# Strided attention and a squared-ReLU layer: where the strided V is spread, and an early load's place in the queue

## The chip, the cores and the metric

The kernel runs on one core of one Trainium2 chip. A core has a matrix engine (TensorE, PE in the profile, with its weight loads as PEld), a vector engine (VectorE, DVE), an activation engine (ScalarE, ACT), a general engine (GpSimd, POOL) and a queue engine that only issues transfers (SyncE, SP). Each engine works through its own instructions in order. Transfers (DMA) are issued from the queues of SP and POOL; those of POOL can change the type on the way, here float32 in memory to bfloat16 on the core. The metric is the device time of one execution in microseconds.

## The reference

For 8 batches and 8 heads of 576 positions with 64 numbers each, the reference computes masked attention: heads 0 to 3 see the last 32 positions ("local"), heads 4 to 7 see earlier positions with the same remainder by 32 ("strided"). Its output, 4608 tokens of 512 numbers, goes through a layer with a squared ReLU.

```
mask_local = (rel >= 0) & (rel < stride)
mask_strided = (rel >= 0) & (pos[None, :] % stride == pos[:, None] % stride)
...
attn = np.exp(scores)
attn = attn / (np.sum(attn, axis=-1, keepdims=True) + 1e-09)
return np.matmul(attn, v).astype(np.float32)
...
h = x @ w_in          # 4608x512 by 512x2048
r = np.maximum(h, 0.0)
g = r * r
return (g @ w_out).astype(np.float32)
```

## The kernel before

Work is cut into 32 units, four per batch: two heads each, the first two units of a batch local, the last two strided. Unit u is of batch u // 4. For each unit the attention goes through steps: T (TensorE transposes q and k, in early batches), S (scores into PSUM banks `pt`, ScalarE takes the exponential into `e`, VectorE multiplies by the mask, L361, or L427 in the paired form SS), D (probabilities by V, L488, then on VectorE a reciprocal L500 and a product L501 into `x_l` or `x_s`; two parts for local, three for strided units), E (transposes x into `xt`).

The layer is cut into 9 chunks of 512 tokens: `mm1(c, i)`, 16 per chunk (L548; ReLU on ScalarE L554; square on VectorE L557 into `g_sb`), and `mm2(c, i)`, 16 per chunk (L588, four matmuls each). A written list of "groups", one mm1 or mm2 each, drives the second part of the kernel, and the attention's steps are put between groups by weights (`due`). `hooks` holds further work by group number: `second(n, ...)` and `at(n, ...)` put a function ahead of group n, after that group's attention steps. The program is emitted in this order, and each engine keeps it.

Strided V needs a layout in which 64 numbers of a position are followed by a column of ones, with a pitch of 72: the tile `vs` (72 partitions x 16 x 72). The data come as dense rows of 512 numbers into `v_st` and are spread from there into `vs` by `cast_v_str` (L255), once for each of the two strided units of a batch.

- Batches 0 and 1 take another way (`load_v_str_first`).
- Batches 2, 3 and 4: one transfer on POOL's queue per batch, float32 to bfloat16 (`load_v_str_sw`, L232); the spreading is on GpSimd, bfloat16 to bfloat16 (`cast_v_str_pair`).
- Batches 5, 6 and 7 (`LB` = 5 on): two float32 transfers on SP's queue (`load_v_str`, L248); GpSimd spreads and casts. The local V of these batches is loaded likewise (`load_v_local`, L216) and cast on GpSimd (`cast_v_local`, L223 and L224).

At group 29 POOL gets a long list: it holds until batch 2's transposes are done (`hold_pool`), issues V of batch 2, q and k rows of batch 3 (`rows(3)`, L133), V of batch 3, the copies of strided q and k of batch 3 (`q_d`, `k_d`, L168), and then spreads V of batches 2 and 3. Two memsets of `vl_st` (L864) follow. At group 51 the same comes for batch 4, with its spreading at group 60.

From batch 5 on, `plan` puts `loads_qk(b)` (loads, the copies `q_d` and `k_d`, casts of q and k on GpSimd, L143) and later `loads_v(b)` at group `n0`. For batches 5, 6 and 7, `n0` is 80, 112 and 144, and `loads_qk` comes at groups 67, 92 and 124.

`v_st` has two buffers and `vs` four slots, so batches b and b + 2 share them.

At the start, `loads_1` issues on POOL's queue: q and k of batch 1's local units, the four quarters of w_out (`load_w_out`, L264) and V of batch 1 among them. Part p of mm2 reads quarter p of w_out; chunk 0 runs its parts in turn for four row blocks, and unit 4's D at group 19 is the first reader of batch 1's local V.

Of the kernel before, what the change touches and what calls it, by code (L numbers as in the profile page):

```python
# [8 lines left out]
FP32 = mybir.dt.float32  # L9
# [5 lines left out]
def kernel(  # L15
# [9 lines left out]
    nc = tc.nc  # L25
    B, H, S, D = q.shape
# [7 lines left out]
    NJ = 8  # L34
    RH = STRIDE // NJ
    SP_ = RH * NA
# [7 lines left out]
    v_st = ctx.enter_context(tc.tile_pool(name="v_st", bufs=2))  # L44
# [54 lines left out]
    units = [(b, p) for b in range(B) for p in range(H // 2)]  # L99
    st = {}  # L100
# [24 lines left out]
    def load_qk_local_sw(b, us, names="qk"):  # L125
        n = 2 * len(us)
        for name, src in (("q", q), ("k", k)):
            if name not in names:
                continue
            t = qk_st.tile([QL, 2, 6 * D], FP32, name=f"{name}_st")  # L130
            t = t.rearrange("p h c -> p (h c)").bitcast(BF16)[:, 0:6 * D * n].rearrange("p (h c) -> p h c", h=n)
            h0 = 2 * units[us[0]][1]
            nc.gpsimd.dma_start(out=t, in_=src[b, h0:h0 + n].rearrange("h (p j) d -> p h (j d)", j=6))  # L133
            for i, u in enumerate(us):
                st.setdefault(u, {})[name + "f"] = t[:, 2 * i:2 * i + 2]

    def cast_qk_local(u, copies, names="qk"):
        s = st[u]
        for name, copy in zip("qk", copies):
            if name not in names:  # L140
                continue
            t = qk_in.tile([QL, 6, 2, D], BF16, name=f"{name}_l")
            copy(t.rearrange("p j h d -> p h j d"),  # L143
                 s[name + "f"].rearrange("p h (j d) -> p h j d", j=6))
            s[name] = t

    def load_qk_str(b, names="qk", room=None):
        for i, (name, src) in enumerate((("q", q), ("k", k))):
            if name not in names:
                continue  # L150
            if room is None:
                t = qk_st.tile([QL, 2, 6 * D], FP32, name=f"{name}_st")
                t = t.rearrange("p h c -> p (h c)").bitcast(BF16).rearrange("p (c x) -> p c x", c=3)
            else:
                t = room[0:QL, 3 * i:3 * i + 3, :]
            nc.gpsimd.dma_start(out=t, in_=src[b, 4:8].rearrange("h (p j) d -> (h p) (j d)", j=NJ)
                                .rearrange("(c r) x -> r c x", r=QL))
            big[b, name] = t
# [6 lines left out]
    def cast_str_dram(b):  # L165
        for name, src in (("q", q), ("k", k)):
            t = dram.tile([4 * SP_, NJ * D], BF16, name=f"{name}_d")
            nc.gpsimd.dma_start(  # L168
                out=t.rearrange("(x y) c -> x (y c)", x=16),
                in_=src[b, H // 2:H].rearrange("h (x y) d -> (h x) (y d)", x=4))  # L170
            big[b, name] = t
# [24 lines left out]
    def transpose_local(u):  # L196
        s = st[u]
        for name in "qk":
            if name == "k":
                full = kTl[v_slot(u)]  # L200
                dst = full[:, 32:32 + S]
            else:
                full = dst = qkT.tile([128, S], BF16, name="qk"[u % 2] + "T")
            nc.sync.dma_start_transpose(out=dst.rearrange("c (t p) -> c t p", p=QL),
                                        in_=s[name].rearrange("p t h d -> p (t h d)"))
            s[name + "T"] = full

    def v_slot(u):
        b, p = units[u]
        return (b * 2 + p % 2) % NV  # L210

    def load_v_local(u, eng):
        b, p = units[u]
        t = vl_sts[p]
        for hh in range(2):
            eng.dma_start(out=t[32:128, NL * hh:NL * (hh + 1), :],  # L216
                          in_=v[b, 2 * p + hh].rearrange("(t p) d -> p t d", p=QL))
        st.setdefault(u, {})["vf"] = t
# [10 lines left out]
    def load_v_str_sw(b):  # L229
        t = v_st.tile([SP_, 2, NJ * D], FP32, name="v_st")  # L230
        t = t.rearrange("p h c -> p (h c)").bitcast(BF16).rearrange("p (h c) -> p h c", h=4)
        nc.gpsimd.dma_start(out=t, in_=v[b, 4:8].rearrange("h (p j) d -> p h (j d)", j=NJ))  # L232
        for i in range(2):
            st.setdefault(4 * b + 2 + i, {})["vf"] = t[:, 2 * i:2 * i + 2]

    def load_v_local_sw(b, u0=0, nu=2):
        i = (2 * b + u0) % NV
        t = vl_all[:, i:i + nu].rearrange("p u h t d -> p (u h t) d")[:, :, 0:D]
        src = v[b, 2 * u0:2 * (u0 + nu)].rearrange("h (t p) d -> p (h t) d", p=QL)
        nc.gpsimd.dma_start(out=t[32:128], in_=src)  # L240
        nc.gpsimd.dma_start(out=t[0:32, 1:2 * nu * NL], in_=src[64:96, 0:2 * nu * NL - 1])
        for u in range(nu):
            st.setdefault(4 * b + u0 + u, {})["v"] = vls[i + u]

    def load_v_str(u, eng):
        b, p = units[u]
        t = v_st.tile([SP_, 2, NJ * D], FP32, name="v_st")
        eng.dma_start(out=t, in_=v[b, 2 * p:2 * p + 2]  # L248
                      .rearrange("h (p j) d -> p h (j d)", j=NJ))
        st.setdefault(u, {})["vf"] = t  # L250

    def cast_v_str(u, copy=None):
        s = st[u]
        t = vss[v_slot(u)]
        (copy or nc.gpsimd.tensor_copy)(t[:, :, 0:D], s["vf"].rearrange("p h (j d) -> p (h j) d", d=D))  # L255
        s["v"] = t

    def load_w_in(i):
# [3 lines left out]
    def load_w_out(i):  # L262
        c = slice(4 * i, 4 * (i + 1))
        nc.gpsimd.dma_start(out=w_out_b[:, c, :], in_=w_out_v[:, c, :])  # L264
# [174 lines left out]
    def load_v_str_first(b):  # L439
        nc.gpsimd.dma_start(  # L440
            out=vs0.rearrange("p u n d -> p (u n d)").rearrange("p (h c) -> p h c", h=4),
            in_=v[b, 4:8].rearrange("h (p j) d -> p h (j d)", j=NJ))
# [223 lines left out]
    def loads_1():  # L666
        load_qk_local_sw(1, (4, 5), "q")
        load_qk_local_sw(1, (4, 5), "k")
        load_w_out(0)
        load_w_out(1)  # L670
        load_v_local_sw(1)
        load_qk_str(1)
        load_w_out(2)
        load_v_str_first(1)
        load_w_out(3)

    def hold_pool(b):
        nc.gpsimd.tensor_copy(held, came[b])

    def cast_v_str_pair(b):  # L680
        for u in (4 * b + 2, 4 * b + 3):
            cast_v_str(u)

    def loads_qk(b):
        for i in range(2):
            load_qk_local(4 * b + i, nc.sync)
        if b == LB:
            hold_pool(b - 1)
        cast_str_dram(b)
        for i in range(2):  # L690
            cast_qk_local(4 * b + i, pool2)

    def loads_v(b):
        for i in range(2):
            load_v_local(4 * b + i, nc.sync)
        for i in range(2):
            load_v_str(4 * b + 2 + i, nc.sync)
        for i in range(2):
            cast_v_local(4 * b + i)
        for i in range(2):  # L700
            cast_v_str(4 * b + 2 + i)

    nc.scalar.preload_act_table_set("natural_log_exp_and_others")
    load_qk_local(0, nc.sync)
# [106 lines left out]
    def at(n, fn):  # L811
        hooks.setdefault(n, []).append(fn)

    def plan(b, g0, g1, n0=None):
        if b < LB:
            at(g0, lambda: transpose_str(b))
            for i in range(2):
                copies = dve2 if b == 2 else (nc.scalar.copy, nc.vector.tensor_copy)
                at(g1 + (4 if b > 2 else 2) * i, lambda u=4 * b + i, c=copies: cast_qk_local(u, c))
            return  # L820
        g = g0 + (g1 - g0) * 45 // 100
        tr, tl = max(g + 8, g0 + (g1 - g0) * 8 // 10), (g + 14, g + 18)
        at(g, lambda: loads_qk(b))
        at(tr, lambda: transpose_str(b))
        at(n0, lambda: loads_v(b))
        for i in range(2):
            at(tl[i], lambda u=4 * b + i: transpose_local(u))

    def second(n, *fns):
        for fn in fns:  # L830
            at(n, fn)

    def D_all(u):
# [23 lines left out]
    rows = lambda b: (lambda: load_qk_local_sw(b, (4 * b, 4 * b + 1)))  # L857
    second(14, rows(2), lambda: cast_str_dram(2))
    plan(2, 28, 28)
    second(29, lambda: hold_pool(2), lambda: load_v_local_sw(2), lambda: load_v_str_sw(2), rows(3),  # L860
           lambda: load_v_local_sw(3), lambda: load_v_str_sw(3), lambda: cast_str_dram(3),
           lambda: cast_v_str_pair(2), lambda: cast_v_str_pair(3))
    for t in vl_sts:
        second(29, lambda t=t: nc.gpsimd.memset(t[0:32], 0.0))  # L864
    done_prev, g_prev = 0, 32
    plan(3, 42, 46)
    second(51, lambda: hold_pool(3), rows(4), lambda: load_v_local_sw(4), lambda: load_v_str_sw(4),
           lambda: cast_str_dram(4))
    second(60, lambda: cast_v_str_pair(4))
    plan(4, 64, 61)  # L870
    for b in range(2, B):
        g_end, s_end = ready.get(b, starts[b]), ends[4 * b + 3]
# [50 lines left out]
```

## Time and profile before

| | us |
|---|---|
| median of 8 runs | 308.86 |
| lowest, highest | 308.46, 310.24 |
| the profiled execution's own time | 310.24 |
| its span, first to last instruction | 308.5 |
| PE busy in the span | 298.9 |
| DVE, ACT, POOL busy | 160.7, 166.1, 74.5 |
| strided V spread on GpSimd, 12 instructions | 6.7 + 7.0 |

The page gives busy times for the whole span. PE's line shows how little it stands; what matters are the places where it does. The table by stages gives each engine's busy time in a stretch; the list of waits tells which engine's instruction ended a wait; the timeline shows single instructions with start and duration, and in brackets the idle time of the engine before it with what ended it. A duration on DVE or POOL can hold time in which the instruction stood and did not work, so the same instruction at two places is worth comparing.

### The profile page before, as it was taken

What the parts mean: (1) busy time and instruction counts of PE and PEld (TensorE: products, weight loads), DVE (VectorE), ACT (ScalarE), POOL (GpSimd) and SP (SyncE); (2) the same over time, 40 slices, a digit from 0 to 9 for tenths busy, and PEclk for the clock granted to TensorE, in tenths of its full rate; (3) what the DMA queues carried; (4) which work ended last, traced back from release to release, by engine and by line L of the source; (5) the groups of instructions that cost most, each with busy time, mean ns of one, the idle gap of its engine ahead of it and who ended that gap; (6) DMA issues with size and microseconds to landing.
All of it is one profiled execution on the core that took longest, in us unless ns stands there. A gap on an engine that the chain in (4) does not pass through costs nothing.

```text
span 308.5 us, 6092 instructions
## 1 busy us (share of the span) xinstructions
PE 298.9 (97%) x2368; PEld 149.3 (48%) x2368; DVE 160.7 (52%) x406; ACT 166.1 (54%) x335; POOL 74.5 (24%) x103
## 2 busy tenths in 40 slices
PE   7989999999999999999999999999999999999995
PEld 2544564544554554445445554444444444444444
DVE  4557656478777875665748586563422222222200
ACT  4748738786577765554646555464434344444311
POOL 8853210664512324440443052000000000000000
PEclk9999999999999999999999999999999999999999
DMA  8999997999999989998999592221230001000121
GB/s 158 149 203 205 189 208 150 224 165 160 139 194 185 214 167 211 187 178 194 214 195 204 122 185 70 72 55 53 83 96 36 34 35 36 34 34 34 59 79 69
DMA packets 85908, 40.74 MB, mean 132 GB/s; under 512 B 69784, under 2 KB 79544, under 8 KB 85688
## 3 DMA queue, kind: packets, MB, share of 16 engines
q1 hardware_dynamic: 59560, 25.37, 36.7%
q0 software_dynamic: 26320, 14.99, 35.7%
q8 instruction: 18, 0.29, 0.4%
q14 instruction: 10, 0.08, 0.1%
HBM read 37.63 MB, written 13.57 MB: 166 GB/s over the span
## 4 chain that ended last, share of the span: by engine, by line
PE 84%; DVE 8%; DMA 4%; ACT 1%; POOL 1%; issue 1%; SPq 0%; DVEq 0%; ACTq 0%
PE ph L548 36%; PE py L588 27%; PE ph L588 6%; PE pt L588 3%; PE pt L488 3%; DMA w_in_b<-in_moe_w_in_dram 3%; DVE g_sb L557 2%; PE pt L347 2%; PE pt L548 1%; DMA k_st<-in_k_dram 1%; DVE x_l L501 1%; PE pt L291 1%; DVE e L361 1%; PE pt L570 1%; DVE k_l L143 1%; DVE x_s L501 1%
## 5 line engine op out<-in xcount | busy, mean ns | idle before, releaser
L548 PE MATMUL ph<-xt,w_in_b 128*128 128x512 bf16 x552 | 139.8, 379 | 0.0
L554 ACT ACTIVATE r<-ph 128x512 bf16<-128x512 f32 x138 | 82.3, 597 | 94.3 <-PE ph L548 92.7
L557 DVE TENSOR_TENSOR g_sb<-r 128x512 bf16<-128x512 bf16 x144 | 65.1, 453 | 104.7 <-ACT r L554 103.8
L588 PE MATMUL py<-w_out_b,g_sb 128*128 128x512 bf16 x400 | 102.7, 379 | 0.0
L548 PEld LDWEIGHTS <-w_in_b 128*128 128x128 bf16 x576 | 52.3, 98 | 55.5 <-DMA w_in_b<-in_moe_w_in_dram 0.7
L588 PEld LDWEIGHTS <-g_sb 128*128 128x128 bf16 x560 | 51.4, 98 | 56.3 <-issue 0.4
L326 ACT ACTIVATE e<-pt 128x288 bf16<-128x288 f32 (+1 forms) x86 | 30.5, 408 | 8.8 <-PE pt L347 8.7
L588 PE MATMUL ph<-w_out_b,g_sb 128*128 128x512 bf16 x112 | 28.2, 379 | 0.0
L488 PEld LDWEIGHTS <-e 128*128 128x128 bf16 (+1 forms) x384 | 20.1, 97 | 15.4 <-DVE e L361 1.1
L592 ACT COPY y<-py 128x512 f32<-128x512 f32 x25 | 14.7, 586 | 6.3 <-PE py L588 6.3
L501 DVE TENSOR_TENSOR x_s<-pt,rinv 72x384 bf16<-72x384 f32 (+1 forms) x33 | 16.7, 505 | 1.1
L501 DVE TENSOR_TENSOR x_l<-pt,rinv 96x384 bf16<-96x384 f32 x25 | 13.8, 554 | 0.9
L500 DVE RECIPROCAL rinv<-pt 96x6 f32<-96x6 f32 (+2 forms) x58 | 10.7, 184 | 5.9 <-PE pt L488 5.7
L223 POOL CAST vl<-vl_st 128x768 bf16<-128x768 f32 x6 | 5.3, 891 | 31.7 <-DMA vl_st<-in_v_dram 20.0
L488 PE MATMUL pt<-vs,e 72*128 72x65 bf16 x174 | 11.1, 194 | 1.3 <-DVE e L361 0.7
L423 ACT ACTIVATE e<-pt 72x504 bf16<-72x504 f32 (+3 forms) x25 | 10.9, 482 | 0.6 <-PE pt L411 0.6
L588 PE MATMUL pt<-w_out_b,g_sb 128*128 128x512 bf16 x48 | 11.2, 379 | 0.0
L255 POOL COPY vs<-v_st 72x1024 bf16<-72x1024 bf16 x6 | 6.7, 1138 | 15.4 <-DMA v_st<-in_v_dram 15.4
L361 DVE TENSOR_TENSOR e<-e,mask_full 128x576 bf16<-128x576 bf16 x20 | 9.0, 450 | 1.8 <-ACT e L326 1.6
L361 DVE TENSOR_TENSOR e<-e,mask_str 72x576 bf16<-72x576 bf16 x16 | 7.8, 494 | 3.8 <-ACT e L326 3.7
L488 PE MATMUL pt<-vl,e 128*128 128x65 bf16 x150 | 8.7, 193 | 0.0
L592 ACT COPY y<-ph 128x512 f32<-128x512 f32 x7 | 4.1, 581 | 7.0 <-PE ph L588 7.0
(132 smaller groups left out, 237.1 us busy)
## 6 DMA issues: line engine op xcount, KB each, us to landing
out_dram<-y SPq DMA_DIRECT2D x35, 256.0 KB, 2.9
w_out_b<-in_moe_w_out_dram POOLq DMA_DIRECT2D x4, 512.0 KB, 14.7
q_d<-in_q_dram POOLq DMA_DIRECT2D x6, 288.0 KB, 8.2
k_d<-in_k_dram POOLq DMA_DIRECT2D x6, 288.0 KB, 9.5
q_st<-in_q_dram SPq DMA_DIRECT2D x12, 144.0 KB, 3.6
k_st<-in_k_dram SPq DMA_DIRECT2D x12, 144.0 KB, 5.7
vl_st<-in_v_dram SPq DMA_DIRECT2D x12, 144.0 KB, 4.1
v_st<-in_v_dram SPq DMA_DIRECT2D x6, 288.0 KB
```

Of the source, the lines that this page charges most:

```text
L255: (copy or nc.gpsimd.tensor_copy)(t[:, :, 0:D], s["vf"].rearrange("p h (j d) -> p (h j) d", d=D))
L326: nc.scalar.activation(e[0:kn, lo:lo + S // 2], pss[row][half][0:kn, 0:S // 2], AF.Exp, scale=scale)
L361: nc.vector.tensor_tensor(x, x, m, op=ALU.mult)
L423: nc.scalar.activation(o, x, AF.Exp, scale=scale)
L488: nc.tensor.matmul(po[:, n - n0, :], e[0:kn, pos(n):pos(n) + 128], rhs[0:kn, src(n), 0:D + 1], start=True, stop=True)
L500: nc.vector.reciprocal(rinv[0:w, 0:m], po[0:w, 0:m, D:D + 1])
L501: nc.vector.tensor_tensor(x, po[0:w, 0:m, 0:D], rinv[0:w, 0:m].to_broadcast([w, m, D]), op=ALU.mult)
L548: nc.tensor.matmul(ph, w_in_b[:, kk, 128 * ff:128 * (ff + 1)], xt[kk][:, 512 * c:512 * (c + 1)], start=(kk == order[0]), stop=(kk == order ...
L554: nc.scalar.activation(r, ph, AF.Relu)
L557: later(1, lambda: nc.vector.tensor_tensor(g[:, ff, :], r, r, op=ALU.mult))
L588: nc.tensor.matmul(py, g[:, ff, 128 * j:128 * (j + 1)], w_out_b[:, ff, :], start=(ff == 0), stop=(ff == 15))
L592: nc.scalar.copy(y, py)
```

## The change

Four edits. `load_v_str` and its six transfers on SP's queue go; batches 5 to 7 use `load_v_str_sw` in `loads_qk`, issued on POOL's queue behind `q_d` and `k_d`. The spreading of all six batches goes from GpSimd to VectorE, one unit per group: batch 2 at groups 43 and 44, batch 3 at 56 and 57, batch 4 at 72 and 73, batches 5 to 7 at `n0 + 1` and `n0 + 2`. At group 29, `rows(3)` goes ahead of batch 2's `load_v_str_sw`. In `loads_1`, V of batch 1's local units goes ahead of w_out's second quarter.

```diff
-    def load_v_str(u, eng):
...
-    def cast_v_str(u, copy=None):
+    def cast_v_str(u, copy):
         s = st[u]
         t = vss[v_slot(u)]
-        (copy or nc.gpsimd.tensor_copy)(t[:, :, 0:D], s["vf"].rearrange("p h (j d) -> p (h j) d", d=D))
+        copy(t[:, :, 0:D], s["vf"].rearrange("p h (j d) -> p (h j) d", d=D))
         s["v"] = t
...
         load_w_out(0)
+        load_v_local_sw(1)
         load_w_out(1)
-        load_v_local_sw(1)
         load_qk_str(1)
...
-    def cast_v_str_pair(b):
-        for u in (4 * b + 2, 4 * b + 3):
-            cast_v_str(u)
...
         cast_str_dram(b)
+        load_v_str_sw(b)
         for i in range(2):
             cast_qk_local(4 * b + i, pool2)
...
         for i in range(2):
             load_v_local(4 * b + i, nc.sync)
         for i in range(2):
-            load_v_str(4 * b + 2 + i, nc.sync)
-        for i in range(2):
             cast_v_local(4 * b + i)
-        for i in range(2):
-            cast_v_str(4 * b + 2 + i)
...
         at(n0, lambda: loads_v(b))
         for i in range(2):
+            at(n0 + 1 + i, lambda u=4 * b + 2 + i: cast_v_str(u, nc.vector.tensor_copy))
             at(tl[i], lambda u=4 * b + i: transpose_local(u))
...
-    second(29, lambda: hold_pool(2), lambda: load_v_local_sw(2), lambda: load_v_str_sw(2), rows(3),
-           lambda: load_v_local_sw(3), lambda: load_v_str_sw(3), lambda: cast_str_dram(3),
-           lambda: cast_v_str_pair(2), lambda: cast_v_str_pair(3))
+    second(29, lambda: hold_pool(2), lambda: load_v_local_sw(2), rows(3), lambda: load_v_str_sw(2),
+           lambda: load_v_local_sw(3), lambda: load_v_str_sw(3), lambda: cast_str_dram(3))
+    for b, n in ((2, 43), (3, 56), (4, 72)):
+        for i in range(2):
+            second(n + i, lambda u=4 * b + 2 + i: cast_v_str(u, nc.vector.tensor_copy))
...
-    second(60, lambda: cast_v_str_pair(4))
```

## The prediction

> **What bounds the kernel now.** First I read the page's busy times: TensorE (PE) is busy for 97% of the span, at a granted clock of 9 tenths or more in every slice.
>
> ```profile
> PE 298.9 (97%) x2368; PEld 149.3 (48%) x2368; DVE 160.7 (52%) x406; ACT 166.1 (54%) x335; POOL 74.5 (24%) x103
> ```
>
> So no engine's sum of work matters, only PE's idle time: 308.5 - 298.9 = 9.6 us. The table by stages places it.
>
> ```profile
> 0.00:30.00 30.00, 26.12 (x262) 13.44 (x263) 17.05 (x58) 18.45 (x39) 19.05 (x34) 1.00 1.19 178
> 66.00:80.00 14.00, 12.69 (x137) 6.68 (x134) 12.17 (x30) 10.32 (x24) 5.57 (x6) 1.00 1.23 159
> 94.00:100.00 6.00, 5.54 (x45) 2.52 (x44) 4.90 (x11) 4.64 (x10) 2.21 (x2) 1.00 1.03 162
> 180.00:187.00 7.00, 6.60 (x71) 3.34 (x68) 6.23 (x15) 3.98 (x8) 6.00 (x6) 1.00 0.93 150
> ```
>
> Columns: stretch, its length, busy time of PE, weight load, VectorE (DVE), ScalarE, GpSimd (POOL). The start has 3.9 us of idle PE and the tail (300 to 308.5, not shown) 3.5; the change reaches neither. Between, 1.31 us is lost in 66-80, 0.46 in 94-100 and 0.40 in 180-187: there DVE is busy for 87, 82 and 89%, and POOL works on elements. PE's waits in those stretches all end on DVE:
>
> ```profile
> PE pt L488 <- DVE e L361: 0.7, 1, 0.7
> PE pt L347 <- DVE x_s L501: 0.6, 1, 0.6
> PE pt L488 <- DVE x_s L501: 0.5, 1, 0.5
> PE pt L411 <- DVE x_s L501: 0.4, 1, 0.4
> ```
>
> The timelines (start, duration) tell why DVE is late. POOL, then DVE, then PE:
>
> ```profile
> 73.16 2.25 POOL L255 COPY vs<-v_st 72x1024 bf16<-72x1024 bf16 x2 [5.19 <-DMA v_st<-in_v_dram]
> 75.36 1.40 POOL L864 MEMSET vl_st<- 32x768 f32 x2
> 95.03 2.21 POOL L255 COPY vs<-v_st 72x1024 bf16<-72x1024 bf16 x2 [8.99 <-DMA v_st<-in_v_dram]
> ```
> ```profile
> 73.45 1.05 DVE L361 TENSOR_TENSOR e<-e,mask_str 72x576 bf16<-72x576 bf16 x1
> 75.60 1.38 DVE L143 COPY k_l<-k_st 96x768 bf16<-96x768 bf16 x1
> 90.40 0.35 DVE L143 COPY k_l<-k_st 96x768 bf16<-96x768 bf16 x1
> 95.42 0.92 DVE L557 TENSOR_TENSOR g_sb<-r 128x512 bf16<-128x512 bf16 x1 [0.71 <-ACT r L554]
> 96.27 1.19 DVE L143 COPY k_l<-k_st 96x768 bf16<-96x768 bf16 x1
> ```
> ```profile
> 74.56 0.30 PE L488 MATMUL pt<-vs,e 72*128 72x65 bf16 x4 [0.74 <-DVE e L361]
> 79.12 0.28 PE L347 MATMUL pt<-qT,kTl 64*128 64x96 bf16 x5 [0.57 <-DVE x_s L501]
> 98.39 0.35 PE L488 MATMUL pt<-vs,e 72*128 72x65 bf16 x6 [0.46 <-DVE x_s L501]
> ```
>
> The same copy takes 0.35 us with POOL idle and 1.38 or 1.19 beside a POOL copy or memset; a mask product takes 1.05 instead of its 0.45, a square 0.92 instead of 0.42. PE then stands.
>
> **The change, part by part.** All durations are of the profiled execution (310.24 us, span 308.5); the median of the eight runs is 308.86, so I carry the difference over to the median and keep a wide range for it.
>
> *Copies of batches 2 to 4 go to DVE.* POOL loses six copies of 1.03 to 1.26 us; DVE gains six. Price of one on DVE: k_l's 0.35 us for 768 columns, by 1024/768, is 0.47 as a whole, and a fixed part would make it less: I take 0.40. Bounds: 0.35 below; above, 1.33 us, if it ran at the 0.75 us per 576 columns of the copies from PSUM. `v_st` and `vs` lie in SBUF in runs of 64 numbers, as k_l's tiles do, so the k_l row is the near one.
>
> Batch 2 (group 43, after unit 8's first x_l, which ends at 67.76) also gains a wait. Its transfer is now issued behind q and k rows of batch 3 (`rows(3)`), so it is fifth in the POOL queue, and lands about where k's rows land now:
>
> ```profile
> k_st<-in_k_dram POOLq DMA_DIRECT2D x1, 288.0 KB, 8.3
> ```
>
> 60.19 + 8.3 = 68.5 (it landed at 58.78 + 6.9 = 65.7). DVE stands from 67.76 to 68.5. Queued behind it: the square of group 43, x_l of unit 8, masks of unit 9, for which PE's L488 at 70.10 waits. I walk DVE's rows on from there, start to start (copy 0.33, square 0.34, reciprocal 0.21, product 0.48, mask 0.36): the first mask of unit 9 ends at 70.7 instead of 69.32 (PE +0.6). The queue stays packed, the idle 0.40 before 71.02 is used up, and mask_str, now 0.45 instead of 1.05, ends at 74.8 instead of 74.50 (PE +0.27). Then k_l costs 0.35 instead of 1.38, since POOL's memsets now follow its DMA issues at 64.5 to 66; x_s of unit 10 ends at 78.3 instead of 79.06, and the bank is free before PE comes. The matmul of 79.12 starts at 78.64: **-0.47**. Bounds: if the data were there at 67.8, PE would gain about 1.2 here (-0.47 - 0.74); each us of later landing costs one us, so +1.0 at a landing of 70.
>
> Batch 3 (groups 56, 57; about 84.0 and 85.0): 0.33 each; DVE's idle 0.34, 0.17 and 0.77 before 85.24, 87.09 and 88.64 covers them. 0, with 0.66 above if that cover were gone, and no gain, as only work is added. Batch 4 (groups 72, 73; about 103.2 and 105.6): idle 0.57, 0.44 and 0.49 before 104.52, 106.43 and 108.75 covers them. 0, above 0.66.
>
> At 94-100 POOL's copies of batch 4 are gone: the square gives back 0.50 and k_l 0.84. The x_s that ends at 98.34 would end near 97.6; PE came at 96.90 + 4 x 0.216 = 97.77 and started at 98.39: **-0.62**, which is all of that wait; 0 is the other bound.
>
> *Batches 5 to 7.* SP loses six issues of 0.30 to 1.09 us, POOL six casts of 1.04 to 1.28 and gains three issues of 0.76; DVE gains six copies of 0.40. Only batch 5 is close: POOL issues at 105.85, behind k_d (105.36 + 6.3 = 111.7 landed), so it lands near 113.2 (1.5 behind, as batch 4's V, 84.23 + 10.7, is behind its neighbour now), and DVE asks at group 81, near 113. Behind it stand a square (four r buffers, eight groups of nearly 1 us of slack) and unit 17's x_l at 115.48; DVE has 0.80 and 0.50 idle before 114.56 and 115.48. 0, above 0.5. The issue pushes q_l and k_l casts of batch 5 by 0.76, of which the waits of 0.32 and 3.81 before 108.30 and 112.94 take all. Batches 6 and 7 land some 10 us ahead of groups 113 and 145. Without POOL's cast at 184.47, DVE's rows up to 186.6 get back 0.14 (square 0.56 at 185.47 against 0.42); the v_l casts at 180.68 stay, but their loads no longer share queues with two v_st loads. Take **-0.2**; bounds 0 and the whole stall, -0.57.
>
> *Start-up.* V of batch 1 lands now at 20.26 + 16.9 = 37.2 and 21.55 + 16.4 = 38.0; L488 reads it at 37.94, with no idle PE. After the swap the queue, which serves in order of issue, brings V by 35.3 and w_out's second quarter by 38.0 instead of 34.5 (19.26 + 15.2). The mm2 of part 1 that reads it starts at 39.49: 1.5 us spare. On POOL each issue waits for the landing eight issues earlier; the waits reshuffle between three neighbours, and q_d's issue at 38.42 stays. 0; bounds -0.1 and, if the transfer slipped 2 us, +0.5.
>
> *Port.* The rows above show that POOL's and DVE's SBUF work excludes. The Trainium skill ("SBUF — State Buffer", section "SBUF: two separate sides") states it as an exclusive lock and speaks against this change: a DVE copy in a 2-port mode also keeps POOL from writing descriptors of its own DMAs, so moving copies to DVE would starve transfers. By this rule the pairs near 84 and 105, which fall among POOL's issues, would hold up some transfers for 0.4 us each; the q_l copy of 0.52 at 30.25, beside an issue, agrees in kind, and nothing of batches 3 and 4 is so urgent. The sum by the rule would be 0 to 0.4 us worse.
>
> Sum: -0.47 - 0.62 - 0.2 = -1.3 us: the profiled execution to 308.9, the median to 307.6.
>
> **The rivals.**
> - *A wider relief, 306.6.* PE also gets the 0.74 of the landing wait back, or small waits vanish too. For it: all four DVE waits lie beside POOL's copies. Against: DVE is 87% busy there and gets two copies more. -1.3 - 0.9.
> - *The stalls only move, 308.8.* The extra DVE work of 6 x 0.40 = 2.4 us up to 106 eats the 0.6 + 1.03 + 0.5 + 0.84 = 3.0 it gets back, or the matmul spared a wait meets the next one. Within 0.2% (0.6 us, what a measurement here can tell from no change).
> - *DVE stands for batch 2's data, 309.8.* For it: DVE already waits 0.74 by my own numbers, and PE needs the masks behind it. It turns the gain of this place to a loss when the landing is 0.47 us later than 68.5, eats all of 1.3 at 69.8, and decides for slower by 0.2% from 70.4; at 70.7 the time is 307.6 + 2.2. Against: five transfers of a queue served in order land at the same total.
> - *w_out's second quarter is late, 309.5.* Needs a slip of 1.5 us before it costs anything, and 3.4 to give +0.6.
> - *The copy is slow on DVE* (1.33 us): batch 2 alone adds 2 x 0.93 and batch 3 some 1.2 past its cover: -1.3 + 3.1, so 310.7. Against: k_l's layout is as broken, and runs in 0.35.
>
> **How the numbers follow.** My forecast 0.45; wider relief 0.16; stalls only move 0.20; batch 2's wait 0.11; w_out 0.03; slow copy 0.05. Faster 0.45 + 0.16 = 0.61, same 0.20, slower 0.19. The range goes from below the wider relief (all of -0.47 - 0.74, -0.62, -0.57 is -2.4: 306.5) to 309.6, a landing of batch 2's data at 70.5, which leaves the worst of the last three cases out. The forecast's own range is 306.9 to 308.2.
>
> **What would show it.** DVE's spread copies at 0.35 to 0.45 us; a DVE wait for v_st of 0.5 to 1 us near 68; mask_str near 74 at 0.45 and k_l near 76 and 96 at 0.35; no PE wait near 79 and 98; PE's idle time in 66-100 down from 1.9 to about 0.8 us. It is wrong if DVE waits over 2 us for v_st, if copies take 1 us, if a wait of PE for w_out_b appears near 39, or if PE's idle time comes back at other DVE waits.

## The result, and the profile after

The changed kernel takes 310.81 us (median of 23 runs, 307.91 to 312.18); the kernel before, run beside it, 308.85 us. The ratio is 1.0053, 95% interval 1.0037 to 1.0069: slower by 0.5%, about 1.6 us, where 1.3 us less was forecast. Of most kernels here some executions, and of a few kernels many, come out 4 to 12 us above the others; the ratios leave these out, and where their number is itself the finding it is given as "executions above 313 us".

The profiled execution, the longest of the 24, took 313.51 us, with a span of 311.8, against 310.24 and 308.5 before. The page's busy times and the granted clock by slices:

```profile
PE 301.1 (97%) x2368; PEld 150.1 (48%) x2368; DVE 162.1 (52%) x418; ACT 166.0 (53%) x335; POOL 64.3 (21%) x94
...
PEclk9999999997999999999999999999999999999999
```

GpSimd has lost the copies (74.5 to 64.3 us), and VectorE gains only 1.4 us net: it got 5.5 us of copies (eleven at 0.41 to 0.42, one at 0.92) and much of that back elsewhere. The digit 7 is new: one slice, 70 to 78 us, at a lower TensorE clock.

The lines that matter among the waits of VectorE, then of TensorE (us in total, times, longest):

```profile
DVE vs L248 <- DMA v_st<-in_v_dram: 3.2, 1, 3.2
```
```profile
PE pt L481 <- DVE e L354: 3.2, 2, 2.8
PE pt L481 <- DVE x_s L494: 0.3, 1, 0.3
PE pt L404 <- DVE x_s L494: 0.2, 1, 0.2
```

L248 is the spreading copy; L354, L481 and L494 are the lines that were L361, L488 and L501. The waits of TensorE between 74 and 99 us are gone, and two of 3.2 us together (2.77 and 0.38) stand in their place. VectorE's timeline, then TensorE's:

```profile
67.16 0.55 DVE L494 TENSOR_TENSOR x_l<-pt,rinv 96x384 bf16<-96x384 f32 x1
70.88 0.42 DVE L248 COPY vs<-v_st 72x1024 bf16<-72x1024 bf16 x1 [3.17 <-DMA v_st<-in_v_dram]
72.58 0.45 DVE L354 TENSOR_TENSOR e<-e,mask_full 128x576 bf16<-128x576 bf16 x1
78.02 0.45 DVE L354 TENSOR_TENSOR e<-e,mask_str 72x576 bf16<-72x576 bf16 x1
79.86 0.35 DVE L143 COPY k_l<-k_st 96x768 bf16<-96x768 bf16 x1
```
```profile
73.09 0.33 PE L481 MATMUL pt<-vl,e 128*128 128x65 bf16 x5 [2.77 <-DVE e L354]
73.79 0.20 PE L481 MATMUL pt<-vl,e 128*128 128x65 bf16 x1 [0.38 <-DVE e L354]
73.83 1.41 PE L541 MATMUL ph<-xt,w_in_b 128*128 128x512 bf16 x4
75.04 1.91 PE L581 MATMUL ph<-w_out_b,g_sb 128*128 128x512 bf16 x4
78.96 1.03 PE L581 MATMUL ph<-w_out_b,g_sb 128*128 128x512 bf16 x4
```

VectorE is done with unit 8's x_l at 67.71 and stands at the copy until V of batch 2 is there; the masks of unit 9, queued behind it, start at 72.58 instead of 68.87, and TensorE stands. Then it computes slowly: four matmuls of 512 columns take 1.91 us, where the same four take 1.03 at 78.96. The windows (stretch, length, busy time of PE, weight load, DVE, ACT, POOL, then granted clock, busy share of the DMA engines, GB/s) put numbers to it:

```profile
70.00:73.00 3.00, 0.31 (x2) 0.00 (x0) 2.08 (x7) 1.33 (x3) 0.00 (x0) 1.00 1.94 217
74.00:77.50 3.50, 3.50 (x15) 1.43 (x14) 2.31 (x8) 1.19 (x3) 0.00 (x0) 0.55 0.27 56
66.00:80.00 14.00, 10.85 (x96) 5.06 (x93) 8.20 (x24) 7.49 (x19) 0.77 (x2) 0.88 1.20 149
94.00:100.00 6.00, 5.91 (x65) 3.22 (x64) 4.26 (x11) 4.13 (x9) 0.00 (x0) 1.00 1.04 169
```

TensorE idles 3.15 us in 66 to 80 (1.31 before): 1.84 more. From 74.34 the clock record shows half clock for 3.41 us, in which half the work, 1.7 us, is lost. In 94 to 100 it idles 0.09 instead of 0.46. The sum, 1.84 + 1.7 - 0.37 = 3.2, is close to the difference of the spans (3.3). The profile of `after_e_late` below, at 311.29 us, has the same picture: VectorE stands 2.40 us for V, which lands at 69.48, and half clock follows for 3.41 us from 73.30.

Of the 24 executions, 11 have a mean granted clock of 0.995 or less, with a median of 311.6 us; the 13 others, at 0.997 or more, have 309.7 (3.41 us at half make a mean of 0.995). So the executions without a half clock are 0.9 us above the kernel before, which is what the stand costs less what the change gains, and somewhat under half are 1.9 us further up. These times do not tell how much of the 1.9 is the half clock and how much a longer stand; in the profile the clock is 1.7.

### The profile page after: what moved, and what is told of

Same layout as the page of the kernel before. It is cut to its first block, busy times and chain, and to the rows that moved or that the text cites. A ratio compares the mean times of both kernels' runs of the same rounds, so it can differ in the third digit from the quotient of the medians.

```text
span 311.8 us, 6089 instructions
## 1 busy us (share of the span) xinstructions
PE 301.1 (97%) x2368; PEld 150.1 (48%) x2368; DVE 162.1 (52%) x418; ACT 166.0 (53%) x335; POOL 64.3 (21%) x94
## 4 chain that ended last, share of the span: by engine, by line
PE 69%; DVE 6%; DMA 4%; POOL 1%; ACT 1%; issue 0%; DVEq 0%; ACTq 0%
PE ph L541 29%; PE py L581 26%; PE ph L581 5%; DMA v_st<-in_v_dram 3%; PE pt L481 3%; PE pt L581 2%; DVE g_sb L550 2%; DMA kT_s<-k_d 1%; PE pt L563 1%; PE pt L340 1%; DVE x_s L494 1%; PE pt L404 1%; DVE x_l L494 1%; DVE vs L248 1%; DVE e L354 1%; PE pt L517 1%
## 5 line engine op out<-in xcount | busy, mean ns | idle before, releaser
L550 DVE TENSOR_TENSOR g_sb<-r 128x512 bf16<-128x512 bf16 x144 | 64.0, 446 | 103.5 <-ACT r L547 102.8
L581 PE MATMUL ph<-w_out_b,g_sb 128*128 128x512 bf16 x112 | 29.4, 392 | 0.0
L481 PEld LDWEIGHTS <-e 128*128 128x128 bf16 (+1 forms) x384 | 20.3, 98 | 18.1 <-DVE e L354 4.0
L494 DVE TENSOR_TENSOR x_s<-pt,rinv 72x384 bf16<-72x384 f32 (+1 forms) x33 | 16.7, 505 | 1.1
L494 DVE TENSOR_TENSOR x_l<-pt,rinv 96x384 bf16<-96x384 f32 x25 | 13.8, 553 | 0.9
L481 PE MATMUL pt<-vl,e 128*128 128x65 bf16 x150 | 9.0, 195 | 3.5 <-DVE e L354 3.2
L481 PE MATMUL pt<-vs,e 72*128 72x65 bf16 x174 | 10.9, 193 | 0.1
L354 DVE TENSOR_TENSOR e<-e,mask_full 128x576 bf16<-128x576 bf16 x20 | 9.0, 451 | 1.5 <-ACT e L319 1.4
L354 DVE TENSOR_TENSOR e<-e,mask_str 72x576 bf16<-72x576 bf16 x16 | 7.6, 480 | 3.8 <-ACT e L319 3.7
L143 POOL CAST q_l<-q_st 96x768 bf16<-96x768 f32 x6 | 5.6, 935 | 18.5 <-DMA q_st<-in_q_dram 18.2
```

The source lines that it names most:

```text
L143: copy(t.rearrange("p j h d -> p h j d"), s[name + "f"].rearrange("p h (j d) -> p h j d", j=6))
L354: nc.vector.tensor_tensor(x, x, m, op=ALU.mult)
L481: nc.tensor.matmul(po[:, n - n0, :], e[0:kn, pos(n):pos(n) + 128], rhs[0:kn, src(n), 0:D + 1], start=True, stop=True)
L494: nc.vector.tensor_tensor(x, po[0:w, 0:m, 0:D], rinv[0:w, 0:m].to_broadcast([w, m, D]), op=ALU.mult)
L550: later(1, lambda: nc.vector.tensor_tensor(g[:, ff, :], r, r, op=ALU.mult))
L581: nc.tensor.matmul(py, g[:, ff, 128 * j:128 * (j + 1)], w_out_b[:, ff, :], start=(ff == 0), stop=(ff == 15))
```

## The experiments

The theory after the comparison: the order of the transfers, V of batch 2 behind the k and q rows of batch 3, makes VectorE stand, and the stand is the whole loss. Against it: the start-up swap, the transfers of batches 5 to 7, the mere work of the copies, and, for the half clock, that the stand alone is the price.

**Which part of the change costs.** `order_back` gives batch 2's V its old place in the queue; the copies and all else stay changed.

```diff
-    second(29, lambda: hold_pool(2), lambda: load_v_local_sw(2), rows(3), lambda: load_v_str_sw(2),
+    second(29, lambda: hold_pool(2), lambda: load_v_local_sw(2), lambda: load_v_str_sw(2), rows(3),
```

> The changed kernel with one edit undone: V of batch 2 is issued ahead of q and k rows of batch 3 again. Theory A (the loss is VectorE standing 3.2 us for batch 2's V, TensorE with it for 3.1 us, and the half clock that follows for 3.4 us, worth 1.7): V lands near 66 to 67, VectorE has no wait for v_st, TensorE's idle time near 70 is under 0.6 us, no half clock near 75; 307.3 to 308.3 us, 0.6 to 1.5 below the kernel before. Theory B (the loss is in the extra VectorE work or in the transfers of batches 5 to 7): stays at 310 to 311.

`spread_later` keeps the new order and asks for the data four groups later.

```diff
-    for b, n in ((2, 43), (3, 56), (4, 72)):
+    for b, n in ((2, 47), (3, 56), (4, 72)):
```

> The changed kernel with batch 2's two copies at groups 47 and 48 instead of 43 and 44; the order of the transfers stays as changed. Theory A: V still lands near 70 to 71, VectorE comes to it at about 72, no wait; 307.0 to 308.3 us. If the order of the transfers itself costs (q and k rows early, or the queue), it stays above 309.

`order_back`: 0.9972 (0.9939 to 1.0004). `spread_later`: 0.9975 (0.9949 to 1.0001). Either edit takes the loss away, so the place of the wait is what costs, and not the copies. A repeat of `order_back` on another chip, below, gives 1.0007 (0.9986 to 1.0029): there too the loss is gone, but a gain over the kernel before is not shown. VectorE in `order_back`:

```profile
66.37 0.55 DVE L494 TENSOR_TENSOR x_l<-pt,rinv 96x384 bf16<-96x384 f32 x1
66.85 0.41 DVE L248 COPY vs<-v_st 72x1024 bf16<-72x1024 bf16 x1
67.18 0.41 DVE L550 TENSOR_TENSOR g_sb<-r 128x512 bf16<-128x512 bf16 x1
```

V landed at 65.07, the copy follows x_l at once, and TensorE idles 0.17 us in 66 to 80:

```profile
66.00:80.00 14.00, 13.83 (x156) 7.68 (x155) 12.61 (x36) 9.90 (x24) 0.00 (x0) 1.00 1.16 149
94.00:100.00 6.00, 6.00 (x57) 3.05 (x55) 4.67 (x14) 5.09 (x11) 0.00 (x0) 1.00 1.30 140
```

But neither is simply a better kernel: 7 of 12 executions of `order_back` and 6 of 12 of `spread_later` are above 313 us, against 1 of 35 of the kernel before and 2 of 12 of `start_only` beside them. This was in no theory; the last group of runs follows it.

`start_only` is the kernel before with the start-up swap alone.

```diff
         load_w_out(0)
-        load_w_out(1)
         load_v_local_sw(1)
+        load_w_out(1)
```

> The kernel before with only V of batch 1 ahead of w_out's second quarter. Theory A and my prediction: V lands near 35, w_out's second quarter near 38, read at 39.5; no change, within 0.3 us of before. Rival: the swap alone makes a part of the loss, 0.6 us or more.

0.999 (0.9966 to 1.0014): no effect. Its trace gave more than was asked. From 66 us on this kernel does what the kernel before does, so its windows are a second sample of the stalls that the change was to remove:

```profile
66.00:80.00 14.00, 12.24 (x132) 6.39 (x131) 12.96 (x30) 9.70 (x23) 5.71 (x6) 1.00 1.25 138
94.00:100.00 6.00, 6.00 (x53) 3.01 (x52) 3.99 (x12) 5.26 (x12) 2.49 (x2) 1.00 1.23 121
180.00:187.00 7.00, 7.00 (x73) 3.66 (x72) 5.51 (x14) 3.82 (x8) 5.23 (x6) 1.00 0.88 182
```

The idle time of 66 to 80 is there again (1.76), that of 94 to 100 and of 180 to 187, 0.46 and 0.40 in the profile of before, is not. POOL copies just as long in 94 to 100 (2.49), but here it does so from 97.51 and meets nothing that TensorE waits for.

`only_567` is the kernel before with batches 5 to 7 changed (transfers on POOL's queue, copies on VectorE); `only_234` is it with batches 2 to 4 spread by VectorE and no transfer moved.

```diff
         cast_str_dram(b)
+        load_v_str_sw(b)
...
-            load_v_str(4 * b + 2 + i, nc.sync)
...
-            cast_v_str(4 * b + 2 + i)
...
+            at(n0 + 1 + i, lambda u=4 * b + 2 + i: cast_v_str(u, nc.vector.tensor_copy))
```
```diff
-           lambda: cast_v_str_pair(2), lambda: cast_v_str_pair(3))
+    for b, n in ((2, 43), (3, 56), (4, 72)):
+        for i in range(2):
+            second(n + i, lambda u=4 * b + 2 + i: cast_v_str(u, nc.vector.tensor_copy))
...
-    second(60, lambda: cast_v_str_pair(4))
```

> The kernel before with the change for batches 5 to 7 alone (one casting transfer per batch on POOL's queue, spread by VectorE at n0 + 1 and n0 + 2). Theory A and my prediction: -0.2 us, within -0.6 to +0.3 of before. Theory B (the loss is in these batches): 1 us or more above before.

> The kernel before with the spreading of batches 2, 3 and 4 alone on VectorE (groups 43, 56, 72), no transfer moved. Theory now: the gain of the change lies here and is free of new waits (V of batch 2 lands near 65 to 66, VectorE comes at 67.8): 0.8 to 1.6 us below before, no executions above 312 beyond before's share. Rival (VectorE's extra work costs as much as POOL's copies did): within 0.3 us of before.

`only_567`: 1.0018 (0.9999 to 1.0037), no gain, and if anything a loss, with 2 of 12 executions above 313 us. `only_234`: 1.0024 (0.9989 to 1.0058), where I had expected 0.8 to 1.6 us below, with 8 of 12 executions above 313 us, so that its ratio rests on a minority and says little. Both profiles fell on long executions (315.49 and 316.32) and are read below.

**What a stand of VectorE costs by itself.** Memsets on VectorE at group 43 of the kernel before, where the copy stands, make its queue late by a known time with no transfer touched; `warm` gives TensorE dummy matmuls at group 46, just ahead of the masks' readers.

```diff
+    for i in range(8):
+        second(43, lambda i=i: nc.vector.memset(xt[1 + i % 3][:, T - 768:T], 0.0))
+    second(46, lambda: warm(12))
```

`delay_short` and `delay_long` have 2 and 4 memsets without the last line, `delay_long_filled` has 4 with it; `delay_8` and `delay_8_filled` are the same pair with 8. `pe_kept_busy` is the changed kernel with `warm(14)`.

> The kernel before, with two memsets of 768 columns (on columns of xt that are free until later, about 0.8 us each) put on VectorE at group 43: VectorE is 1.6 us late at the place where it waits in the changed kernel, without any change of a transfer. Both theories: TensorE stands about 1 us near 70, no half clock, 0.5 to 1.6 us above before.

> The same with four memsets (3.2 us, the length of VectorE's wait in the changed kernel). If a stand of TensorE of this length also costs a stretch of half clock (3.4 us at half, 1.7 us lost), it is up to 3.3 us above the two memsets, more than the 1.6 us of added VectorE work, with a half clock near 75 in the profile; if standing costs only its own length, it is 1.6 above them, clock 1.0.

> The four memsets, and 12 matmuls of 512 columns on zeros (2.6 us of thrown away TensorE work) ahead of group 46's mm1, in the time in which TensorE would stand. If the half clock comes of standing, the clock stays at 1.0 and the time is up to 1.7 us below the four memsets alone; if not, it is the same or above.

> The kernel before with eight memsets at group 43 on VectorE: they took 0.40 us each in the runs with two and four, so 3.2 us in all. TensorE stands about 2.9 us near 70. If a stand of this length costs a half clock as well, 1.6 above the four memsets (which gave +1.4) and 1.7 more: 4 to 5 us above before, half clock near 75. If it costs its own length alone: 2.7 to 3.3 above before, clock 1.0.

> The eight memsets, with 12 matmuls of 512 columns on zeros (2.6 us) ahead of group 46's mm1, where TensorE would stand. If the half clock comes of standing: clock 1.0 near 75, 2.7 to 3.5 above before, so up to 1.7 below eight memsets alone. If not: the same as eight memsets alone or above.

> The changed kernel with 14 matmuls of 512 columns on zeros (14 x 0.216 = 3.0 us of TensorE work that is thrown away) put ahead of group 46's mm1, just before the place where TensorE stands in the changed kernel. VectorE's wait is untouched. If the half clock after the wait comes from the standing and is worth 1.7 us, the clock stays at 1.0 through 74 to 78 and the time is 1 to 2 us below the changed kernel's 310.8: about 309.3. If the half clock is no consequence of the standing or costs nothing, the time is 310.8 or above (in executions in which the wait is short the added work costs up to 3 us).

One memset took 0.40 us and not 0.8: the trace shows it as 384 numbers of 32 bits. So the first three runs were half as strong as planned, and the pair with 8 was run for that reason.

| run | VectorE late by, us | ratio (95%) | mean clock |
|---|---|---|---|
| delay_short | 0.8 | 1.003 (1.0012 to 1.0049) | 0.998 or more, but for one of 12 |
| delay_long | 1.6 | 1.0048 (1.0032 to 1.0064) | 0.998 or more, but for one of 12 |
| delay_long_filled | 1.6 | 1.0087 (1.0069 to 1.0105) | 0.998 or more |
| delay_8 | 3.2 | 1.0169 (1.0135 to 1.0204) | 0.987 to 0.995 |
| delay_8_filled | 3.2 | 1.0113 (1.0085 to 1.0142) | 0.998 or more |
| pe_kept_busy | as after | 1.0061 (1.004 to 1.0082) | 0.997 or more |

The first two steps are near one us per us: 0.9 and 1.5 us of time for 0.8 and 1.6 of delay. 3.2 us of delay cost 5.2 (1.69% of 308.9). The trace of `delay_8`, VectorE, TensorE, and windows:

```profile
68.76 3.23 DVE L864 MEMSET xt<- 128x384 uint32 x8
```
```profile
73.38 0.46 PE L488 MATMUL pt<-vl,e 128*128 128x65 bf16 x5 [2.67 <-DVE e L361]
```
```profile
70.00:73.00 3.00, 0.71 (x4) 0.10 (x1) 2.85 (x9) 1.73 (x4) 0.00 (x0) 0.99 1.75 232
73.00:77.00 4.00, 3.38 (x13) 1.36 (x14) 2.94 (x9) 0.94 (x3) 2.50 (x3) 0.50 0.37 75
77.00:80.00 3.00, 3.00 (x28) 1.23 (x26) 1.60 (x5) 0.24 (x1) 1.19 (x2) 0.54 1.02 164
```

TensorE stands 2.67 us, as in the changed kernel, and then runs at half clock, for 6.83 us by the clock record. With the dummy matmuls in the hole there is no half clock, and although they are work on top, the kernel is faster: 312.1 against 314.8 us in the median, and 1.9 us in the mean (95% interval 0.4 to 3.4, six executions each). That is the test that the clock is a cost of its own. For the stand of 1.6 us the same matmuls only cost (311.8 against 310.4): nothing was to be saved there, the trace shows waits of 0.95 and 0.38 us at that place and no half clock. `pe_kept_busy` missed its expectation: the dummies took the half clock away in all 12 executions, but the median was 310.62. In its profile V landed at 69.43, so the stand was shorter than the dummy work that was to fill it; on the changed kernel the price of the clock was not separated this way.

The Trainium skill ("TensorE: Matmul & The Clock Gate", section "Part 1: The HAM clock gate (the "warmup" mystery)") says that the array falls to 4/8 of its clock after at least one idle window of about 3.4 us that runs freely. The stretches of 3.41 and 6.83 us at half are one and two such windows. But the stands ahead of them were shorter than the page's window: the longest waits are 2.77, 2.02 and 2.67 us in the changed kernel, `after_e_late` and `delay_8`, with 0.25 to 0.38 more close behind, and 3.19 and 2.75 in `only_234` and `only_567` below. And length alone does not decide, for `back_and_late5` has a TensorE wait as long as the first and full clock throughout:

```profile
PE ph L541 <- DMA xt<-x_l: 2.7, 1, 2.7
```
```profile
PEclk9999999999999999999999999999999999999999
```

The clock records tell what does. Counted from where the clock first rises, every later change in the 20 profiles comes after a whole number of stretches of 3.413 us; the drops to half behind a stand come after 20 (changed kernel, `after_e_late`, `delay_8`), 30 (`only_234`) and 35 (`only_567`). In the stretch just ahead of these five drops TensorE was busy for 26, 35, 35, 13 and 38% of the time. In every other stretch at full clock up to 298 us, in all 20 profiles, it was busy for 51% or more, and the clock stayed. The 2.73 us of `back_and_late5` (143.31 to 146.04) lie across the end of a stretch at 144.48, so that the two stretches are still 66 and 55% busy. On this record, then, some 2.1 us without work in one stretch are enough (62% of 3.413), and 2.73 us are harmless when two stretches share them; where between 38 and 51% the bound lies is not measured. This fits a window that runs freely, and would explain why 11 of 24 executions pay and 13 do not, but each kernel has one profile, so that for the single executions it is argued and not shown.

**Why the relieved kernels have long executions.** In the long profiles the damage is 30 to 50 us further on. `only_234`, waits of VectorE and TensorE, and windows:

```profile
DVE vs L255 <- DMA v_st<-in_v_dram: 4.8, 1, 4.8
```
```profile
PE pt L347 <- DVE x_s L501: 3.2, 1, 3.2
PE pt L347 <- DMA kTl<-k_l: 1.8, 1, 1.8
PE pt L488 <- DVE e L361: 1.5, 1, 1.5
```
```profile
94.00:98.00 4.00, 4.00 (x36) 1.84 (x33) 2.57 (x8) 3.58 (x7) 0.00 (x0) 1.00 1.33 76
98.00:102.00 4.00, 4.00 (x37) 2.22 (x36) 3.22 (x9) 3.26 (x7) 0.00 (x0) 1.00 1.66 81
102.00:106.00 4.00, 4.00 (x34) 2.04 (x32) 1.51 (x4) 2.91 (x5) 0.00 (x0) 1.00 1.30 40
106.00:110.00 4.00, 0.81 (x14) 0.38 (x12) 1.69 (x6) 0.90 (x2) 0.00 (x0) 0.94 0.88 57
```

From 94 to 106 the DMA engines' share (the last column but one) is 1.3 to 1.7, and they move 40 to 81 GB/s; in `order_back`'s normal profile the share is 1.1 to 1.4, and after 81 GB/s in 94 to 98 they move 207 and 190 in 98 to 102 and 102 to 106. Batch 4's V lands at 108.25 instead of 94.9, the queue's hold for batch 5 ends at 115.5 instead of 104.4, and TensorE idles 3.2 us. In `only_567` the same puts off batch 5:

```profile
120.86 1.41 DVE L255 COPY vs<-v_st 72x1024 bf16<-72x1024 bf16 x2 [7.97 <-DMA v_st<-in_v_dram]
```

What differs ahead of it is when SP starts the transposing DMAs of unit 12's x (`xt<-x_l` of `step_E`), counted from the end of POOL's issue of batch 4's k rows: 8.9 us after it in the changed kernel, 6.7 in the kernel before; 3.9 in `back_and_late5`, 4.0 in `only_234` and 4.5 in `only_567`, the three profiles with a late hold (111.0, 115.5, 110.1). `order_back` (4.6), its repeat (4.9) and `spread_later` (5.2) had normal profiles with holds at 104.2, 104.7 and 104.8: an early start makes the jam possible and not certain. My reading is that the earlier TensorE is, the earlier these transposes come, into transfers that still run; no long execution of `order_back` itself was profiled.

Two ways to take them out of there: `order_back_te` lets TensorE transpose x of units 12 and 13, and `order_back_e_late` issues the two DMAs some 7 us later. `order_back_2` repeats `order_back`; `before_te` has TensorE's route in the kernel before; the ones with `late5` ask for the copies of batches 5 to 7 sixteen groups later; `after_e_late` is the changed kernel with the later issue.

```diff
-        if local and b >= XB:
+        if local and b >= XB and u not in (12, 13):
```
```diff
-                order.append(E_(u - 1))
+                order.append((lambda: None) if u - 1 in (12, 13) else E_(u - 1))
...
+    second(64, E_(12), E_(13))
     plan(4, 64, 61)
```
```diff
-            at(n0 + 1 + i, lambda u=4 * b + 2 + i: cast_v_str(u, nc.vector.tensor_copy))
+            at(n0 + 17 + i, lambda u=4 * b + 2 + i: cast_v_str(u, nc.vector.tensor_copy))
```

> The changed kernel with V of batch 2 ahead of q and k rows of batch 3 again, and the copies of batches 5, 6 and 7 at 16 groups later (97, 129, 161 and one after). Theory now: the changed kernel has two places where VectorE stands for a transfer, batch 2's V at group 43 and batch 5's at group 81; with the first mended alone, TensorE comes to the second earlier and the wait there grows, up to the 8.0 us seen with batches 5 to 7 alone. With both mended no VectorE wait for v_st is left, no half clock, 307.3 to 308.3 us in the median of all executions. Rival (executions above 313 came from something else on the chip): a third or more of them is again above 313.

> order_back, with x of units 12 and 13 (the local units of batch 3) transposed on TensorE and copied by VectorE, and not by SP's DMA. Theory C (a gain of TensorE brings these DMA transposes into the time of batch 4's transfers, which then land up to 14 us late): POOL's hold for batch 5 ends before 106, at most 1 of 12 executions above 313, median 307.8 to 308.8 (TensorE gets 0.5 us of transposes more). Rival (something else delays the transfers): 4 or more of 12 above 313, as before.

> The control: order_back as it was, on this chip. Theory C and the rival: 4 to 8 of 12 executions above 313. If it has none here, the late transfers were a matter of the other chip, and the comparison says nothing.

> The kernel before with units 12 and 13 transposed on TensorE. Theory C: its price alone, 0 to 0.8 us above before (12 transposes of 96 columns, 0.5 us of TensorE, and two copies of about 0.75 on VectorE), no more executions above 313 than before.

> order_back_te with the copies of batches 5 to 7 at 16 groups later. No VectorE wait for v_st is left. Within 0.4 us of order_back_te if batch 5's wait at group 81 is covered by the r buffers as I predicted, 0.5 to 1.5 below if it is not.

> The changed kernel with V of batch 2 issued ahead of the k and q rows of batch 3, and with SP's transposing DMAs of the x of units 12 and 13 issued some 7 us later, ahead of the transposes of batch 4, and not by TensorE. If what makes some executions of the kernel with that order long is that these transposes run into batch 4's transfers on the DMA engines, 0 or 1 of 12 executions are above 313 us, the transposes start more than 9 us behind POOL's issue of batch 4's k rows, and the time is 307.5 to 308.2, 0.6 to 1.4 below the kernel before. If what helped was only that TensorE did the transposing, so that the DMA engines had less work in all, 3 to 7 of 12 stay above 313.

> The changed kernel with nothing but SP's transposing DMAs of the x of units 12 and 13 issued some 7 us later. V of batch 2 stays behind the k and q rows of batch 3, so VectorE stands for it at group 43 as before. If that stand alone makes the changed kernel slower, the time is 310.0 to 311.3, as without the edit. If the transposes beside batch 4's transfers take part in it, it is 308.5 to 309.5.

| run | ratio (95%) | executions above 313 us |
|---|---|---|
| back_and_late5 | 1.0102 (1.0069 to 1.0136) | 2 of 6 |
| order_back_te | 1.0005 (0.9984 to 1.0026) | 0 of 12 |
| order_back_2 | 1.0007 (0.9986 to 1.0029) | 3 of 12 |
| before_te | 1.0035 (1.0016 to 1.0055) | 0 of 12 |
| order_back_te_late5 | 1.0013 (0.9991 to 1.0035) | 0 of 12 |
| order_back_e_late | 1.0017 (0.999 to 1.0045) | 0 of 12 |
| after_e_late | 1.0036 (1.0003 to 1.0068) | 1 of 10 |

`order_back` and its repeat have 10 long executions of 24; with the two transposes out of the way, by either route, there are none in 36. On one and the same chip it is 3 of 12 against 0 of 24; `order_back_e_late` ran on another chip, without `order_back` beside it. In it the same DMAs run, later (10.6 us behind the issue), so as far as 12 executions tell it is their place and not the load that counts. Its time missed the expectation of 307.5 to 308.2: 308.92, two executions with a clock below 0.995, and a TensorE wait of 0.82 at 90.4 behind a copy of k. `back_and_late5` missed too, and told that a late copy for batch 5 is no cure. `after_e_late` falls between its two theories (309.84 over all ten, four of them at a clock of 0.993 or less, and a VectorE stand of 2.40 us again); it settles nothing beyond that moving the transposes leaves the stand where it is.

TensorE's route costs 1.1 us by itself (`before_te`, 309.93), more than the 0 to 0.8 I had put; against that, `order_back_te` is at 309.04: the change without the wait is worth 0.9 us there (1.0 in the mean, interval 0.5 to 1.5), while `order_back_2` is level with the kernel before. No version here is clearly faster than the kernel before.

## Why the prediction was wrong

The forecast's direction was wrong, and the rival "DVE stands for batch 2's data" is what happened: "decides for slower by 0.2% from 70.4", and V landed at 70.86 in the profile. The sign that the prediction named for it, a VectorE wait of over 2 us for v_st, is there (3.17). It gave 309.8 for a landing at 70.7; the median is 310.81, above the range. The executions without half clock have 309.7: the rival, too, had no price for the clock.

- **The step that failed: "lands about where k's rows land now ... 68.5".** That 68.5 was one landing in one execution. Over the 20 profiles of this study the fifth transfer of that queue, whichever it is, lands at 68.3 to 70.9 us, 11.9 to 13.8 us after the hold that opens the queue; the profile of before has the shortest of these, 11.9. In the changed kernel the hold ended 0.8 later (57.39 for 56.59) and the five took 13.5. Where V is fifth, four profiles give 68.94, 69.43, 69.48 and 70.86. My own price, one us per us, held where VectorE was delayed by 0.8 and 1.6 us (`delay_short`, `delay_long`); the argument "five transfers of a queue served in order land at the same total" looked at the order and not at the spread, and gave 0.11 to a case that needed 1.9 us of it.
- **A term that was not there: the clock.** No row of before showed half clock behind a stand, and the sum had no term for it. It is 1.7 us in the profile; 11 of 24 executions have it.
- **The relief in 66 to 80: right.** mask_str took 0.45 and k_l 0.35, and the waits at 79 and 98 are gone. Without the landing wait I had written that TensorE "would gain about 1.2 here"; `order_back` has 0.17 us of idle time there, for 1.31 in before (1.76 in `start_only`, 0.51 in `before_te`).
- **-0.62 at 94 to 100 and -0.2 at 180 to 187: mostly not there to be gained.** The mechanism (a POOL copy stretches VectorE) is right, but `start_only`, whose work in these two stretches is that of the kernel before, has no TensorE idle time in either. Of six others of which that nearly holds (`before_te` and the five delays), five idle for 0.06 us or less in 94 to 100 and `delay_8` for 1.23; none idles for more than 0.16 in 180 to 187. So for the most part the stalls belonged to the profiled execution of before, at 310.24 the longest of its eight. The bound of -0.57, "the whole stall", was also too wide: that stretch idles 0.40. How much there was to be had stays open: 0.9 by `order_back_te` against `before_te`, nothing by `order_back_2` and by `only_567` (1.0018).
- **Copy price, start-up, batches 3 to 5: right.** 0.40 was taken, 0.41 to 0.42 measured, in all but the one beside POOL's casts; `start_only` is at 0.999; no TensorE idle time from 80 to 94, where batch 3's are; batch 5's V landed at 114.96 and not 113.2, but VectorE, late by then, came 2.4 us after it. Where VectorE is not late it does stand for this V: 2.23, 2.08, 2.49 and 2.72 us in `order_back`, its repeat, `spread_later` and `order_back_e_late`. TensorE is busy for all of 110 to 126 in these four, so the cover that I counted on (the square's buffers) holds. `order_back_te_late5`, meant to test this, does not: in `order_back_te` V landed at 112.78 and there was no wait to take away. And the cover is gone once batch 4's transfers are late (`only_567`).
- **Port.** VectorE beside POOL's casts near batch 4's copies:

```profile
106.40 1.39 DVE L550 TENSOR_TENSOR g_sb<-r 128x512 bf16<-128x512 bf16 x1
107.72 0.41 DVE L248 COPY vs<-v_st 72x1024 bf16<-72x1024 bf16 x1
109.08 0.92 DVE L248 COPY vs<-v_st 72x1024 bf16<-72x1024 bf16 x1
```

The Trainium skill ("SBUF — State Buffer", section "SBUF: two separate sides") states an exclusive lock between the two engines on a pair of ports that they share, and the rows agree (0.92 for 0.41, 1.39 for 0.42). Of it 0.3 us reached TensorE, as the wait for x_s at L481 (0.31 at 111.27), within the bound of 0.66 that stood for batch 4. By the rule of that section against this change the copies would keep POOL from writing the descriptors of its transfers. In `order_back` two copies meet POOL's issues of batch 4 (at 82.05 and 83.14): they took 0.63 and 0.71 us, while the issues beside them (0.68, 1.18, 0.74) took as long as in the changed kernel (0.68, 1.18, 0.74), where no copy lies beside them. So in these rows it was the copy that stood; what the transfers themselves lost was not isolated.

## What to carry to other kernels

A copy that moves to an in-order engine brings the wait for its data with it, in front of all that is queued there. Place it by the spread of the landing, of which one profile shows one value, and price a stall only if a second profile has it too. A hole of 2 to 3 us in TensorE can cost 1.7 us or more on top of its length in clock, and an engine that comes early may bring its own transfers into others that were clear of it.

## What the runs showed of the hardware

TensorE's clock fell to half, for 3.41 or 6.83 us, in a kernel that is otherwise at full clock, whenever TensorE was busy for 38% or less of one of the 3.413 us stretches that follow each other from where the clock first rises (five drops in 20 profiles, the tail left out), and never where it was busy for 51% or more; waits of 2.02 and 0.38 us inside one stretch did it, one of 2.73 us across two did not.

Two transposing DMAs of SP that started 3.9 to 4.5 us behind the issue of batch 4's k rows on POOL's queue went, in three profiles, with a landing of batch 4's V 8 to 13 us later than the 94.9 of the kernel before; in three with 4.6 to 5.2 us it landed at 95.9 to 96.5. With the two moved to 10.6 us behind, or taken out, no execution of 36 was above 313 us. Why the DMA engines move so little in the late profiles stays open.
